# A two-layer transformer on one core: the softmax sums divided out per head group instead of per pair of groups, layer-norm copies kept in their stream, and seven planner constants changed

## The chip, the cores and the metric

The kernel runs on one core of a Trainium2 chip. The metric is the device time of one execution in microseconds (us); three executions of the kernel before took 896.95, 897.54 and 895.75 us, median 896.95. TensorE is called PE (its weight loads PEld), VectorE DVE, ScalarE ACT, GpSimd POOL, and the queue from which SyncE issues transfers SP.

## The reference

Two layers with shared weights; each layer is attention and then a feed-forward block, both with layer norm ahead of them and a residual around them. The sequence has 2048 rows of width 448; there are 16 heads of 28 columns; the hidden width is 1792.

```python
x = x + A(layernorm(x), A_wqkv, A_wo)
x = x + B(layernorm(x), B_w1, B_b1, B_w2, B_b2)
x = x + A(layernorm(x), A_wqkv, A_wo)
x = x + B(layernorm(x), B_w1, B_b1, B_w2, B_b2)

# A: q, k, v = split(x @ wqkv); p = softmax(q @ k.T * 28 ** -0.5); return (p @ v) @ wo
# B: h = relu(x @ w1 + b1); return (h * h) @ w2 + b2
```

## The kernel before, in words

**Order of the work.** The order of instructions on every engine is written by a planner (`Planner`, lines 124 to 214) that runs while the program is built. Each piece of work is an `Op` with an engine, an estimated duration, dependencies and buffers that it acquires (`acq`) and releases (`rel`). Ops stand in streams, and of one stream only the next Op can be chosen. The planner takes, again and again, the Op with the earliest possible start, and among equals that of the stream with the lowest number: 0 for scores, 1 for the exponentials on ACT, 2 for probabilities times values, 3 for normalization, 3.5 (`EV`) for copies out of PSUM, 4 and more for the chains described below. On the chip each engine then works through its queue in exactly this order.

**Attention.** The queries are cut into blocks of 256 rows (list `blocks`, line 242); the last 256 rows of layer 1 are two blocks of 128. A pass is one block of queries, one group of four heads, and a range of keys. Its score tiles of 128x512 are called units here; there are 2048 units over both layers, some 32 to a whole pass. `s_stream` (line 745) takes three units at a time into one PSUM tile of 1536 columns; `e_stream` (line 824) takes their exponential on ACT in one instruction (L833); `p_stream` (line 931) multiplies by the values (L981), whose fifth row block of ones gives the softmax sums as well, and evicts the result (L1004, L1006).

**Units on DVE.** Where `apart` (line 703) allows it, the third unit of a group goes to DVE, which computes the exponential with a polynomial: one instruction at L891, three at L908, one at L903 and the closing one at L914, which frees the scratch set. ACT then has a group of 1024 columns. `apart` refuses when fewer than `STOP` units are left, when no scratch set is free, or when DVE was busy over the last 12 planned us for more than a share `BUSY` = 0.95; the share is `LOW` = 0.6 when `behind` (line 688) says that the chains lag behind a line through the units given by `LINES` and `MARGIN`. The rest of a unit (`a_rest`) starts at a late priority and is raised to `V_LAST` = 1.8, ahead of `p_stream`, once `V_AGE` groups have gone by or once the scores have gone `V_PAST` units beyond the end of the unit's pass (line 897).

**Normalization.** When a pass ends its block and group, the result `oT_sb` holds 28 rows of values and a row of sums for each of four heads. Ahead of the last block of a layer, the sums go by DMA into a tile `dn` spread over 128 partitions (`spread`, L1079), are inverted on DVE (L1084), go to DRAM (`away`, L1090), come back broadcast to the rows of each head as `rec` (`back`, L1098), and DVE multiplies (L1103). `norm_pair` does this for two groups together, from one `oT_sb` tile with both; there are 30 such pairs. The last block of a layer goes through `norm_stream`: a matmul with `sel` copies the sums to all rows (L1046), then come a reciprocal (L1052) and a multiply (L1057).

**Chains.** When all four groups of a block are normalized, `chain` (line 1115) does its output projection, residual, layer norm, hidden layer (L1156 is the ReLU, L1160 the square) and second matrix; in layer 0 the next layer's Q, K and V follow. In `layernorm` the transposed rows are copied out of PSUM (L505); this copy is a stream of its own with number `EV` (line 508). PSUM gives `R_m`, two banks that accumulators, projections and transposes share.

**Buffers.** There are 11 tiles of exponentials (`NPT`), `NOS` tiles of `oT_sb`, and two of `rec`.

Of the kernel before, what the change touches and what calls it, by code (L numbers as in the profile page):

```python
# [11 lines left out]
DT = mybir.dt  # L12
AF = mybir.ActivationFunctionType
ALU = mybir.AluOpType
P = 128
# [20 lines left out]
DCLK = 0.2  # L36
OWN = 2
HALF = 320
LINES = ((280, 1312, 7.8), (1440, 2040, 7.0))
MARGIN = 2.0  # L40
LOW = 0.6
TURNS = 1
ENDU = 100
# [12 lines left out]
V_PRIO = 6.0  # L56
V_LATE = 3.6
V_LAST = 1.8
V_AGE = 6
V_PAST = 2  # L60
OWN3 = 0
FIRST = 90
V_FIRST = 9.2
# [7 lines left out]
BUSY = 0.95  # L71
SPAN = 12.0
NPT = 11
NOS = 3
AEND = 8
HOT = 0.9
MORE = 3
# [8 lines left out]
THIRD = 1  # L86
NL = 0
NLP = 3.8
STOP = 90
HSTOP = 0  # L90
CHUNK = 2
EV = 3.5
# [125 lines left out]
def kernel(  # L218
# [187 lines left out]
    def bank(o, name):  # L406

        if o.res in R_m:
            return ps_m[R_m.index(o.res)].tile([P, 512], DT.float32, name=name, tag="m")[:, :]
        return ps_sc.tile([P, 3 * 512], DT.float32, name="sc", tag="sc")[:, 0:512]  # L410


    def pools_now(early=False):
        return (*R_m, R_sc) if early or len(s_left) == 0 else R_m
# [39 lines left out]
    def layernorm(t0, nt, deps_of, early=False, mv=None, place=None):  # L454
# [26 lines left out]
        xnT = box["x"]  # L481
        ends = []
        todo = []

        def turn(p0, own, xs):
            box = {}

            def tr(e, xs=xs):
                tp = bank(t, "tp").bitcast(DT.bfloat16).rearrange("p (c q) -> p c q", c=NDC)
                box["t"] = tp  # L490
                for k, (xn, _) in enumerate(xs):
                    for dc in range(NDC):
                        nc.tensor.transpose(out=tp[:, dc, k * P:(k + 1) * P],
                                            in_=xn[:, dc * P:(dc + 1) * P], identity=ident[:, :])
            t = Op("PE", 0.07 * NDC * len(xs), tr, deps=[x[1] for x in xs],
                   acq=pools_now(early) if early else spare(1))
            yield t

            def ev(e, p0=p0, w=len(xs) * P):
                tp = box["t"]  # L500
                dst = xnT[:, :, p0 * P:p0 * P + w]
                if e == "ACT":
                    nc.scalar.copy(out=dst, in_=tp[:, :, 0:w])
                else:
                    nc.vector.tensor_copy(out=dst, in_=tp[:, :, 0:w])  # L505
            o = Op("DVE", 0.12 + 0.3 * len(xs), ev, deps=[t], rel=t, sets=[("xT", t0 + p0)] if early else ())
            ends.append(o)
            pl.spawn(EV, iter([o, Op("DVE", 0.0, None, deps=[t], rel=own)]))

        wide = 1 if single else 2  # L510
        for p0 in range(0, nt, wide):
# [18 lines left out]
            while todo:  # L530
                p0, own, xs = todo.pop(0)
                yield from turn(p0, own, xs)
        return xnT, own_xt, ends

    def mm_tile(subs, evac, ev_dur, deps, any_engine=False, sets=(), early=False, post=(), acq=None):
# [343 lines left out]
    def a_unit(gi, x, src, unit, l):  # L879
# [14 lines left out]
                apart_from(gi, t)  # L894
        c = Op("DVE", 0.69, take, deps=[("s", gi)], acq=sets_of(unit), rel=x)
        yield c
        pl.spawn(lambda now: V_LAST if e_now[1] - gi >= V_AGE or at[0] > ends_at[unit[0]] + V_PAST else V_LATE if now > c.end + V_WAIT else V_PRIO if gi > FIRST else V_FIRST, a_rest(gi, c, box, unit, (b0, b1, b2, b3)))

    def a_rest(gi, c, box, unit, bs):
        b0, b1, b2, b3 = bs  # L900
# [24 lines left out]
        yield o  # L925

    norm_done = {}
    pairs = {}
    oTn_of = {}

    def p_stream():


        for pi, (l, qb, g, kbs, first, last) in enumerate(passes):
# [58 lines left out]
                yield o  # L993
            res = {}
            def ev(e, box=box, first=first, last=last, g=g, res=res, n=n, l=l, qb=qb):
                pair = pairs.get((l, qb, g // 2))
                src = box["t"][:, 0:n]
                if last:
                    dst = res["t"] = pair["t"][:, g % 2, :]
                    dst = dst[:, 0:n]  # L1000
                else:
                    dst = part(l, qb, g)
                if first:
                    nc.vector.tensor_copy(out=dst, in_=src)  # L1004
                else:
                    nc.vector.tensor_tensor(out=dst, in0=src, in1=part(l, qb, g), op=ALU.add)  # L1006
            if last and (l, qb, g // 2) not in pairs:
                def both(e, l=l, qb=qb, g=g):
                    pairs[l, qb, g // 2]["t"] = osp.tile([P, 2, QR], DT.float32, name="oT_sb")
                pairs[l, qb, g // 2] = {"own": Op("DVE", 0.0, both, acq=R_os), "ev": [], "res": []}  # L1010
                yield pairs[l, qb, g // 2]["own"]
            pair = pairs[l, qb, g // 2] if last else None
            oe = Op("DVE", 0.15 + n / 930, ev, deps=[o], rel=box["o"])
            yield oe
            if last:
                pair["ev"].append(oe)
                pair["res"].append((g, res))
                if qb == len(blocks[l]) - 1:
                    pl.spawn(3, norm_stream(l, qb, g, res, oe, pair))
                elif len(pair["ev"]) == 2:  # L1020
                    pl.spawn(3, norm_pair(l, qb, g - g % 2, pair))

    def norm_start(l, qb):
        if (l, qb) not in oTn_of:
            def take(e):
                oTn_of[l, qb][0] = np_.tile([P, G, QR], DT.bfloat16, name="oTn")
            oTn_of[l, qb] = [None, Op("DVE", 0.0, take, acq=R_on)]
            yield oTn_of[l, qb][1]

    def norm_end(l, qb, m, gs):  # L1030

        norm_done.setdefault((l, qb), []).extend([m] * gs)
        if len(norm_done[l, qb]) == G:
            pl.spawn(LASTP if (l, qb) == (1, len(blocks[1]) - 1) else NLP + 0.1 * (qb - len(blocks[1])) if l == 1 and qb >= len(blocks[1]) - NL else 4 + 0.1 * qb, chain(l, qb))

    def norm_stream(l, qb, g, res, oe, pair):


        t0, nt = blocks[l][qb]
        n = nt * P  # L1040
        box = {}
        yield from norm_start(l, qb)

        def den(e):
            box["t"] = bank(d, "den")
            nc.tensor.matmul(box["t"][:, 0:n], lhsT=sel[:, :], rhs=res["t"][:, 0:n], start=True, stop=True)  # L1046
        d = Op("PE", 0.1 + n * 4 / 2400, den, deps=[oe], acq=pools_now())
        yield d

        def rcp(e):  # L1050
            box["r"] = rp.tile([P, 2, QR], DT.float32, name="rec")[:, 0, :]
            nc.vector.reciprocal(out=box["r"][:, 0:n], in_=box["t"][:, 0:n])  # L1052
        r = Op("DVE", n * 0.0066, rcp, deps=[d], rel=d, acq=R_rec)
        yield r

        def mul(e):
            nc.vector.tensor_tensor(out=oTn_of[l, qb][0][:, g, 0:n], in0=res["t"][:, 0:n],  # L1057
                                    in1=box["r"][:, 0:n], op=ALU.mult)
        m = Op("DVE", 0.13 + n / 930, mul, deps=[r, oTn_of[l, qb][1]])
        yield m  # L1060
        yield Op("DVE", 0.0, None, deps=[m], rel=r)
        pair.setdefault("mul", []).append(m)
        if len(pair["mul"]) == 2:
            yield Op("DVE", 0.0, None, deps=[m], rel=pair["own"])
        norm_end(l, qb, m, 1)

    def norm_pair(l, qb, g, pair):


        n = blocks[l][qb][1] * P  # L1070
        box = {}
        yield from norm_start(l, qb)
        w = n // DHP
        both = pair["t"][:, :, 0:n]

        def spread(e):
            box["d"] = sp.tile([P, 2, QR // DHP], DT.float32, name="dn")
            for i in range(2):
                nc.sync.dma_start(out=box["d"][:, i, 0:w], in_=both[DH::DHP, i, :])  # L1079
        d1 = Op("DMA", 0.9, spread, deps=pair["ev"], lat=1.0)  # L1080
        yield d1

        def rcp(e):
            nc.vector.reciprocal(out=box["d"][:, :, 0:w], in_=box["d"][:, :, 0:w])  # L1084
        r1 = Op("DVE", 0.33, rcp, deps=[d1])
        yield r1

        def away(e):
            box["s"] = dp.tile([P, 2 * w], DT.float32, name=f"scr{w}")[:, :].rearrange("p k -> (p k)")
            nc.sync.dma_start(out=box["s"].rearrange("(i p j) -> p i j", i=2, p=P), in_=box["d"][:, :, 0:w])  # L1090
        d2 = Op("DMA", 0.4, away, deps=[r1], lat=-0.5)
        yield d2

        def back(e):
            box["r"] = rp.tile([P, 2, QR], DT.float32, name="rec")
            for i in range(2):
                src = box["s"][i * P * w:(i + 1) * P * w].rearrange("(h k) -> h k", h=G)
                nc.sync.dma_start(out=box["r"][:, i, 0:n], in_=src.unsqueeze(1).to_broadcast([G, DHP, n]))  # L1098
        r = Op("DMA", 0.9, back, deps=[d2], acq=R_rec, lat=2.7)
        yield r  # L1100

        def mul(e):
            nc.vector.tensor_tensor(out=oTn_of[l, qb][0][:, g:g + 2, 0:n], in0=both,  # L1103
                                    in1=box["r"][:, :, 0:n], op=ALU.mult)
        m = Op("DVE", 0.13 + 2 * n / 930, mul, deps=[r, oTn_of[l, qb][1]], rel=pair["own"])
        yield m
        yield Op("DVE", 0.0, None, deps=[m], rel=r)
        norm_end(l, qb, m, 2)

    def add_to_x(tb, lo=0, hi=D):  # L1110
        def f(e, t):
# [149 lines left out]
```

## Time and profile before

| What | Value |
|---|---|
| median of three executions | 896.95 us |
| profiled execution, its own time | 896.95 us |
| its span, first to last instruction | 895.2 us |
| ACT busy | 876.9 us (98%) |
| DVE busy | 794.5 us (89%) |
| PE busy | 832.6 us (93%) |
| granted TensorE clock | 0.998 |
| exponentials on ACT with 1536 / 1024 columns | 555 / 128 |
| units computed on DVE | 127 |

Busy time is the union over an engine's instructions; consecutive ones overlap, so that the sum of single durations is larger than the busy time. Idle time of an engine that does not set the end costs nothing. Scores are repeated as filler on PE where the planner expects it to have room, so PE's busy time is not all needed work.

### The profile page before, as it was taken

The page shows a single profiled execution, that of the slowest core. Times are in us where ns is not written, and L with a number is a line of the kernel's source. Part 1 is how long each engine was busy: PE and PEld are TensorE (multiplying, and loading weights), DVE is VectorE, ACT ScalarE, POOL GpSimd, SP SyncE. Part 2 cuts the span into 40 slices and gives each one's busy share as a digit, 9 for nine tenths or more (in the row PEclk, how much of TensorE's full clock was granted, in tenths as well). Part 3 has the DMA queues.
Part 4 walks back from the last instruction along what each step waited for, and adds up shares of the span by engine and source line. Part 5 has one row for each costly group of instructions (what it writes and reads, how often), then busy time and mean ns, then how long its engine had stood idle before and what let it go on. Part 6 is the DMA issues. An engine that isn't in the chain of part 4 may idle for free.

```text
span 895.2 us, 29099 instructions
## 1 busy us (share of the span) xinstructions
PE 832.6 (93%) x12829; PEld 459.1 (51%) x12829; DVE 794.5 (89%) x1575; ACT 876.9 (98%) x704; POOL 39.0 (4%) x98
## 2 busy tenths in 40 slices
PE   8999999999999999999989998888999999999998
PEld 4555654554545545454454554444544544545566
DVE  7988999999889999999999999899898999989654
ACT  8999999999999999999999999999999999999994
POOL 3100000000000000100000000001000000000000
PEclk9999999999999999999999999999999999999999
DMA  9100100000000000000000000011000000000100
GB/s 259 41 3 3 27 17 12 14 14 15 14 2 15 15 14 14 12 10 9 2 1 3 2 2 2 3 39 39 14 13 19 20 25 24 15 10 17 32 19 13
DMA packets 33916, 18.43 MB, mean 21 GB/s; under 512 B 18875, under 2 KB 33340, under 8 KB 33789
## 3 DMA queue, kind: packets, MB, share of 16 engines
q1 hardware_dynamic: 33788, 16.58, 6.6%
q8 instruction: 100, 1.64, 0.8%
q14 instruction: 28, 0.22, 0.1%
HBM read 14.26 MB, written 2.07 MB: 18 GB/s over the span
## 4 chain that ended last, share of the span: by engine, by line
ACT 69%; issue 12%; PE 12%; DVE 5%; DMA 1%; SPq 1%; POOL 0%; DVEq 0%; ACTq 0%
ACT pt L833 69%; PE sc L809 4%; PE mt L553 4%; PE oT L981 3%; PE sc L553 1%; DMA rec<-scr 1%; DVE v_h L908 1%; DVE r L1156 1%; DVE st L448 1%; DVE K_sb L908 1%; DMA x_sb<-in_A_x_dram 0%; PE mt L1210 0%; SPq L303 0%; DVE oTn L1103 0%; DVE x_sb L1112 0%
## 5 line engine op out<-in xcount | busy, mean ns | idle before, releaser
L833 ACT ACTIVATE pt<-sc 128x1536 bf16<-128x1536 f32 (+1 forms) x683 | 863.9, 1565 | 2.9 <-PE sc L809 2.4
L809 PE MATMUL sc<-Q_sb,K_sb 32*128 32x256 bf16 (+1 forms) x5848 | 325.3, 265 | 53.5 <-ACT pt L833 47.3
L809 PEld LDWEIGHTS <-K_sb 32*128 32x128 bf16 x5848 | 157.5, 92 | 229.9 <-issue 200.9
L981 PE MATMUL oT<-pt,V_sb 128*32 128x256 bf16 (+1 forms) x4094 | 152.9, 269 | 0.6 <-DVE xnT L505 0.3
L553 PE MATMUL mt<-xnT,w 128*128 128x256 bf16 (+1 forms) x896 | 119.0, 271 | 1.9 <-DVE xnT L505 0.8
L981 PEld LDWEIGHTS <-V_sb 128*32 128x32 bf16 x4352 | 92.2, 96 | 46.7 <-issue 43.1
L908 DVE SCALAR_TENSOR_TENSOR K_sb<-K_sb 128x512 f32<-128x512 uint16 x165 | 112.9, 684 | 0.9 <-PE mt L553 0.2
L908 DVE SCALAR_TENSOR_TENSOR v_h<-v_h,v_i 128x512 f32<-128x512 f32 x144 | 98.2, 682 | 0.6
L553 PEld LDWEIGHTS <-w 128*128 128x128 bf16 x952 | 78.6, 98 | 36.5 <-issue 28.1
L1156 DVE TENSOR_SCALAR r<-mt 128x512 bf16<-128x512 f32 x106 | 72.2, 681 | 15.1 <-PE mt L553 14.8
L553 PE MATMUL mt<-w,V_sb 128*128 128x448 bf16 (+1 forms) x274 | 66.7, 352 | 0.0
L891 DVE TENSOR_SCALAR v_i<-sc 128x512 int32<-128x512 f32 x72 | 49.3, 685 | 9.7 <-PE sc L809 9.3
L1112 DVE TENSOR_TENSOR x_sb<-x_sb,mt 128x448 bf16<-128x448 bf16 (+1 forms) x63 | 38.2, 610 | 13.5 <-PE mt L553 13.5
L908 DVE SCALAR_TENSOR_TENSOR v_h<-v_i 128x512 f32<-128x512 uint16 x72 | 49.1, 682 | 0.5
L470 POOL TENSOR_TENSOR ve<-mv,eps_t 128x2 f32<-128x2 f32 (+1 forms) x34 | 8.8, 260 | 842.2 <-DVE mv L449 842.2
L1210 PE MATMUL mt<-xn,ident 128*128 128x448 bf16 x130 | 43.5, 357 | 0.5 <-DVE x_sb L1112 0.3
L891 DVE TENSOR_SCALAR K_sb<-sc 128x512 int32<-128x512 f32 x55 | 37.6, 684 | 5.5 <-PE sc L809 5.3
L448 DVE BATCH_NORM_STATS2 st<-x_sb 128x6 f32<-128x448 bf16 x64 | 39.4, 615 | 2.0 <-DMA x_sb<-in_A_x_dram 1.8
L553 PEld LDWEIGHTS <-V_sb 128*128 128x128 bf16 x302 | 24.8, 98 | 25.7 <-issue 11.2
L1160 DVE TENSOR_TENSOR V_sb<-r 128x512 bf16<-128x512 bf16 (+1 forms) x73 | 30.2, 414 | 2.8 <-ACT r L1154 2.2
L914 DVE SCALAR_TENSOR_TENSOR V_sb<-v_h,v_e 128x512 bf16<-128x512 f32 x46 | 31.3, 682 | 0.3
L553 PE MATMUL mt<-wo,oTn 128*128 128x448 bf16 x128 | 30.5, 355 | 0.1
(103 smaller groups left out, 734.8 us busy)
## 6 DMA issues: line engine op xcount, KB each, us to landing
rec<-scr SPq DMA_DIRECT2D x56, 128.0 KB
x_sb<-in_A_x_dram SPq DMA_DIRECT2D x8, 224.0 KB
out_dram<-x_sb SPq DMA_DIRECT2D x15, 112.0 KB
w<-in_B_w_dram SPq DMA_DIRECT2D x1, 1568.0 KB
w<-in_B_w_dram SPq DMA_DIRECT2D x1, 1344.0 KB
dn<-oT_sb SPq DMA_DIRECT2D x56, 4.0 KB
V_sb<-in_A_wqkv_dram SPq DMA_DIRECT2D x4, 168.0 KB
scr<-dn SPq DMA_DIRECT2D x28, 8.0 KB
```

The costliest lines, as they stand in the source:

```text
L448: nc.vector.bn_stats(out=st[:, :], in_=x_sb[:, t0 + j, :])
L553: nc.tensor.matmul(box["t"][:, c0:c0 + n], lhsT=lhsT() if callable(lhsT) else lhsT, rhs=rhs, start=a, stop=b)
L809: nc.tensor.matmul(dst[k][:, i * nt * P:(i + 1) * nt * P], lhsT=K_sb[l][rows, g, (kb + i) * P:(kb + i + 1) * P], rhs=Q_sb[rows, g, t0 * P: ...
L833: t = nc.scalar.activation(out=pt[:, 0:n], in_=gbuf[gi]["sc"][:, 0:n], func=AF.Exp, scale=float(np.log(2.0)) * 2.0 ** -FRAC)
L891: t = nc.vector.tensor_scalar(out=box["i"], in0=two(src), scalar1=EXP_BIAS, scalar2=EXP_LOW, op0=ALU.add, op1=ALU.max)
L908: nc.vector.scalar_tensor_tensor(out=box["h"], in0=box["f"] if begin else box["h"], scalar=b, in1=box["f"], op0=ALU.add, op1=ALU.mult)
L914: nc.vector.scalar_tensor_tensor(out=box["two"](pd), in0=box["h"], scalar=b0, in1=box["e"].bitcast(DT.bfloat16), op0=ALU.add, op1=ALU.mult)
L981: nc.tensor.matmul(box["t"][DHP * hh:DHP * hh + DHP, 0:n], lhsT=V_sb[l][:, kb + i, 4 * g + hh, :], rhs=p[:, c0:c0 + n], start=begin and kb ...
L1112: nc.vector.tensor_tensor(out=x_sb[:, tb, lo:hi], in0=x_sb[:, tb, lo:hi], in1=t[:, 0:hi - lo], op=ALU.add)
L1156: nc.vector.tensor_scalar(out=r[:, 0:w], in0=t[:, 0:w], scalar1=0.0, scalar2=None, op0=ALU.max)
L1160: nc.vector.tensor_tensor(out=h[:, 0:w // n, :], in0=r, in1=r, op=ALU.mult)
L1210: nc.tensor.matmul(t[:, 0:D], lhsT=ident[:, :], rhs=xns[0][:, 0:D], start=True, stop=True)
```

## The change

Three things change.

1. `norm_pair` goes; `norm_stream` serves all blocks. Ahead of the last block of a layer each group has its own spread, reciprocal, away, back and multiply, on tiles of half the size. `osp` has `NOS` = 4 tiles of one group in place of 3 tiles of two.
2. In `layernorm` the copies out of PSUM are yielded at the end of the layer norm's own stream, with that stream's number, and no longer spawned with number 3.5.
3. Constants: `LINES` for layer 0 from 7.8 to 8.0 blocks, `MARGIN` 2.0 to 4.0, `V_AGE` 6 to 5, `V_PAST` and its condition removed, `NOS` 3 to 4, `STOP` 90 to 80.

```diff
-LINES = ((280, 1312, 7.8), (1440, 2040, 7.0))
-MARGIN = 2.0
+LINES = ((280, 1312, 8.0), (1440, 2040, 7.0))
+MARGIN = 4.0
-V_AGE = 6
-V_PAST = 2
+V_AGE = 5
-NOS = 3
+NOS = 4
-STOP = 90
+STOP = 80
...
             ends.append(o)
-            pl.spawn(EV, iter([o, Op("DVE", 0.0, None, deps=[t], rel=own)]))
+            evs.extend([o, Op("DVE", 0.0, None, deps=[t], rel=own)])
...
+        yield from evs
         return xnT, own_xt, ends
...
-        pl.spawn(lambda now: V_LAST if e_now[1] - gi >= V_AGE or at[0] > ends_at[unit[0]] + V_PAST else V_LATE if now > c.end + V_WAIT else ...
+        pl.spawn(lambda now: V_LAST if e_now[1] - gi >= V_AGE else V_LATE if now > c.end + V_WAIT else ...
...
-            oe = Op("DVE", 0.15 + n / 930, ev, deps=[o], rel=box["o"])
+            oe = Op("DVE", 0.15 + n / 930, ev, deps=[o], rel=box["o"], acq=R_os if last else None)
             yield oe
             if last:
-                pair["ev"].append(oe)
-                pair["res"].append((g, res))
-                if qb == len(blocks[l]) - 1:
-                    pl.spawn(3, norm_stream(l, qb, g, res, oe, pair))
-                elif len(pair["ev"]) == 2:
-                    pl.spawn(3, norm_pair(l, qb, g - g % 2, pair))
+                pl.spawn(3, norm_stream(l, qb, g, res, oe))
...
+            def spread(e):
+                box["d"] = sp.tile([P, QR // DHP], DT.float32, name="dn")
+                nc.sync.dma_start(out=box["d"][:, 0:w],
+                                  in_=res["t"][DH::DHP, 0:n])
+            d1 = Op("DMA", 0.5, spread, deps=[oe], lat=1.0)
+            yield d1
+            def rcp(e):
+                nc.vector.reciprocal(out=box["d"][:, 0:w], in_=box["d"][:, 0:w])
+            r1 = Op("DVE", 0.25, rcp, deps=[d1])
+            yield r1
+            def away(e):
+                box["s"] = dp.tile([P, w], DT.float32, name=f"scr{w}")
+                nc.sync.dma_start(out=box["s"][:, :], in_=box["d"][:, 0:w])
+            d2 = Op("DMA", 0.4, away, deps=[r1], lat=-0.5)
+            yield d2
+            def back(e):
+                box["r"] = rp.tile([P, QR], DT.float32, name="rec")
+                src = box["s"][:, :].rearrange("(h a) j -> h (a j)", h=G)
+                nc.sync.dma_start(out=box["r"][:, 0:n], in_=src.unsqueeze(1).to_broadcast([G, DHP, n]))
+            r = own = Op("DMA", 0.5, back, deps=[d2], acq=R_rec, lat=2.7)
+            yield r
         def mul(e):
             nc.vector.tensor_tensor(out=oTn_of[l, qb][0][:, g, 0:n], in0=res["t"][:, 0:n],
                                     in1=box["r"][:, 0:n], op=ALU.mult)
-        m = Op("DVE", 0.13 + n / 930, mul, deps=[r, oTn_of[l, qb][1]])
+        m = Op("DVE", 0.13 + n / 930, mul, deps=[r, oTn_of[l, qb][1]], rel=oe)
```

More of the change, by code (lines that the diff above doesn't have):

```diff
@@ L483, in layernorm @@
         todo = []
+        evs = []
         def turn(p0, own, xs):
@@ L896, in a_unit @@
         yield c
-        pl.spawn(lambda now: V_LAST if e_now[1] - gi >= V_AGE or at[0] > ends_at[unit[0]] + V_PAST else V_LATE if now > c.end + V_WAIT else V_PRIO if gi > FIRST else V_FIRST, a_rest(gi, c, box, unit, (b0, b1, b2, b3)))
+        pl.spawn(lambda now: V_LAST if e_now[1] - gi >= V_AGE else V_LATE if now > c.end + V_WAIT else V_PRIO if gi > FIRST else V_FIRST, a_rest(gi, c, box, unit, (b0, b1, b2, b3)))
     def a_rest(gi, c, box, unit, bs):
@@ L927 @@
     norm_done = {}
-    pairs = {}
     oTn_of = {}
@@ L995, in ev @@
             def ev(e, box=box, first=first, last=last, g=g, res=res, n=n, l=l, qb=qb):
-                pair = pairs.get((l, qb, g // 2))
                 src = box["t"][:, 0:n]
                 if last:
-                    dst = res["t"] = pair["t"][:, g % 2, :]
+                    dst = res["t"] = osp.tile([P, QR], DT.float32, name="oT_sb")
                     dst = dst[:, 0:n]
@@ L1006, in ev, with norm_stream @@
                     nc.vector.tensor_tensor(out=dst, in0=src, in1=part(l, qb, g), op=ALU.add)
[L1007 to L1012, printed above, removed]
-            oe = Op("DVE", 0.15 + n / 930, ev, deps=[o], rel=box["o"])
+            oe = Op("DVE", 0.15 + n / 930, ev, deps=[o], rel=box["o"], acq=R_os if last else None)
             yield oe
             if last:
-                pair["ev"].append(oe)
-                pair["res"].append((g, res))
-                if qb == len(blocks[l]) - 1:
-                    pl.spawn(3, norm_stream(l, qb, g, res, oe, pair))
-                elif len(pair["ev"]) == 2:
-                    pl.spawn(3, norm_pair(l, qb, g - g % 2, pair))
-    def norm_start(l, qb):
+                pl.spawn(3, norm_stream(l, qb, g, res, oe))
+    def norm_stream(l, qb, g, res, oe):
+        t0, nt = blocks[l][qb]
+        n = nt * P
+        box = {}
+        tail = qb == len(blocks[l]) - 1
         if (l, qb) not in oTn_of:
@@ L1028, in norm_start, with den, rcp @@
             yield oTn_of[l, qb][1]
[L1030 to L1054, printed above, removed]
+        if tail:
+            def den(e):
+                box["t"] = bank(d, "den")
+                nc.tensor.matmul(box["t"][:, 0:n], lhsT=sel[:, :], rhs=res["t"][:, 0:n], start=True, stop=True)
+            d = Op("PE", 0.1 + n * 4 / 2400, den, deps=[oe], acq=pools_now())
+            yield d
+            def rcp(e):
+                box["r"] = rp.tile([P, QR], DT.float32, name="rec")
+                nc.vector.reciprocal(out=box["r"][:, 0:n], in_=box["t"][:, 0:n])
+            r = Op("DVE", n * 0.0066, rcp, deps=[d], rel=d, acq=R_rec)
+            own = r
+            yield r
+        else:
+            w = n // DHP
+            def spread(e):
[4 more added lines that the diff above has]
+            yield d1
+            def rcp(e):
+                nc.vector.reciprocal(out=box["d"][:, 0:w], in_=box["d"][:, 0:w])
[7 more added lines that the diff above has]
+            def back(e):
+                box["r"] = rp.tile([P, QR], DT.float32, name="rec")
+                src = box["s"][:, :].rearrange("(h a) j -> h (a j)", h=G)
+                nc.sync.dma_start(out=box["r"][:, 0:n], in_=src.unsqueeze(1).to_broadcast([G, DHP, n]))
+            r = own = Op("DMA", 0.5, back, deps=[d2], acq=R_rec, lat=2.7)
+            yield r
@@ L1058, in mul @@
                                     in1=box["r"][:, 0:n], op=ALU.mult)
-        m = Op("DVE", 0.13 + n / 930, mul, deps=[r, oTn_of[l, qb][1]])
+        m = Op("DVE", 0.13 + n / 930, mul, deps=[r, oTn_of[l, qb][1]], rel=oe)
         yield m
[L1061 to L1108, printed above, removed]
@@ L1110, in add_to_x @@
+        yield Op("DVE", 0.0, None, deps=[m], rel=own)
+        norm_done.setdefault((l, qb), []).append(m)
+        if len(norm_done[l, qb]) == G:
+            pl.spawn(LASTP if (l, qb) == (1, len(blocks[1]) - 1) else NLP + 0.1 * (qb - len(blocks[1])) if l == 1 and qb >= len(blocks[1]) - NL else 4 + 0.1 * qb, chain(l, qb))
     def add_to_x(tb, lo=0, hi=D):
```

## The prediction

> **What bounds the kernel now.** I read the page's engine totals and its chain of waits first, then the waits of ACT, then the groups with their shapes kept apart, then windows and stretches in order of time.
>
> ```profile
> PE 832.6 (93%) x12829; PEld 459.1 (51%) x12829; DVE 794.5 (89%) x1575; ACT 876.9 (98%) x704; POOL 39.0 (4%) x98
> ...
> ACT 69%; issue 12%; PE 12%; DVE 5%; DMA 1%; SPq 1%; POOL 0%; DVEq 0%; ACTq 0%
> ...
> L833 ACT ACTIVATE pt<-sc 128x1536 bf16<-128x1536 f32 (+1 forms) x683 | 863.9, 1565 | 2.9 <-PE sc L809 2.4
> ```
>
> The exponentials keep ACT busy for 863.9 us of 895.2, and ACT stood idle ahead of them for 2.9 us in all. So the time is three parts: an opening of some 20 us, a body in which ACT never waits, and an end after the last exponential. The body shortens only when units go to DVE.
>
> ```profile
> L833 ACT ACTIVATE pt<-sc 128x1536 bf16<-128x1536 f32 x555 | 775.8, 1644 | 2.8 <-PE sc L809 2.4 <-ACT pt L833 0.2
> L833 ACT ACTIVATE pt<-sc 128x1024 bf16<-128x1024 f32 x128 | 147.6, 1223 | 0.1
> L1103 DVE TENSOR_TENSOR oTn<-oT_sb,rec 128x512 bf16<-128x512 f32 x28 | 19.1, 684 | 1.6 <-DMA rec<-scr 1.6
> L1084 DVE RECIPROCAL dn<-dn 128x16 f32<-128x16 f32 x28 | 6.8, 244 | 0.9 <-DMA dn<-oT_sb 0.9
> L1057 DVE TENSOR_TENSOR oTn<-oT_sb,rec 128x256 bf16<-128x256 f32 x4 | 1.6, 410 | 0.0
> L1084 DVE RECIPROCAL dn<-dn 128x8 f32<-128x8 f32 x2 | 0.4, 188 | 0.0
> ```
>
> Neighbours overlap, so a price is the distance from one start to the next. In order of time, ACT near the end and DVE in the body:
>
> ```profile
> 834.13 44.27 ACT L833 ACTIVATE pt<-sc 128x1536 bf16<-128x1536 f32 x33
> ```
>
> ```profile
> 506.50 0.68 DVE L891 TENSOR_SCALAR K_sb<-sc 128x512 int32<-128x512 f32 x1
> 507.09 0.68 DVE L908 SCALAR_TENSOR_TENSOR v_h<-v_i 128x512 f32<-128x512 uint16 x1
> 507.69 0.42 DVE L903 TENSOR_SCALAR v_e<-v_i 128x512 int16<-128x512 int16 x1
> 508.03 0.68 DVE L571 TENSOR_SCALAR Q_sb<-mt 128x512 bf16<-128x512 f32 x1
> ```
>
> A wide exponential costs 44.27/33 = 1.34 us; the 128 narrow ones share 863.9 - 555 x 1.34 = 119 us, 0.93 each. One unit more on DVE makes one wide group narrow and saves 0.41 us. A unit costs DVE five instructions of 0.60 and one of 0.33: 3.3 us.
>
> The windows say how much DVE has left:
>
> ```profile
> 20.00:834.00 814.00, 761.07 (x11542) 412.89 (x11533) 746.83 (x1452) 812.48 (x646) 28.11 (x68) 1.00 0.06 15
> ...
> 800.00:840.00 40.00, 37.82 (x696) 21.63 (x694) 32.92 (x63) 40.00 (x33) 0.00 (x0) 1.00 0.09 25
> ```
>
> Columns are PE, PEld, DVE, ACT and POOL busy. DVE works 746.83 of 814 us (91.7%) in the body, near the planner's cap of 95%. DVE is therefore the second bound: each 3.3 us that the change takes from it costs ACT 0.41.
>
> **Part one: one group at a time.** Per pair, DVE now has a 512-wide multiply and a 16-wide reciprocal (0.60 + 0.16, start to start), afterwards two 256-wide multiplies and two 8-wide reciprocals (256-wide copies and multiplies start 0.33 apart, the 8-wide reciprocal of 856.94 us was followed after 0.12): 2 x 0.45 = 0.90, so 0.14 more. Thirty pairs: 4.2 us, 1.3 units, **+0.5 us**. Bounds: 0 if it falls into DVE's idle 67 us; by full durations (684 + 244 against 2 x 410 + 2 x 188, 0.27 each) 8 us, 2.4 units, +1.0.
>
> [...]
>
> On SP a pair issues two spreads, one away and two backs; afterwards it is two of each: 30 issues more, of 0.36 us (`scr` at 582.82), some 11 us over the run. No engine but DVE waits on these: 1.6 us for `rec`, 0.9 for `dn`. But SP issues in order, and an `away` that waits for a reciprocal holds back the spread of the next group. I take 0 and keep the bound in the third rival. NOS gives four groups in flight, where there were six.
>
> **Part two: the layer-norm copies, V_AGE and V_PAST.** The 34 copies at L505 (0.60 each) had number 3.5, ahead of late units (3.6) and chains; with 4 and up they stand behind both, and the transposed rows hold one of the two shared PSUM banks meanwhile. Behind each queue the hidden matmuls, then the ReLUs on DVE. In the opening they compete only with projections' evictions of 0.6 us and under; I take 0 there, bounds -0.3 and +0.6. A unit of a finished pass was raised when the scores were two units past its end; now only its age raises it, five groups, some 6.3 us. `p_stream` waits for it, behind that the accumulator's bank and its eviction on DVE. Against that, units that end no pass are raised one group (1.27 us) sooner and free their scratch set sooner. No row prices this. What it moves is the share of DVE in use: one percent of 814 us is 8.1 us, 2.4 units, 1.0 us. Bounds: up to the 95% cap, 3.3 percent, less the 4.2 us of part one, -2.7 us; two percent lost, +2.0. I take one percent lost, **+1.0**, since two of the three edits put waiting work later.
>
> **Part three: lines, margin, STOP.** Units pass at 2048/858 = 2.4 per us from 20 us on. By 480 us layer 0 has run some 50 ReLUs (7 a block), so between 6.4 and 7 blocks; its line stands at 6.1 before and after (7.8 x 0.793 - 2/20.2, 8 x 0.793 - 4/20.2): no effect, 0. In layer 1 at 800 us there are 35 ReLUs, 4.6 to 5 blocks, and the line falls from 4.78 to 4.64: here it bites. Chains may lag 2 counts more before DVE units are refused, and STOP lets units start 10 units (4 us) later. DVE in 800 to 840 us has 32.92 busy, 3.9 under the mean 36.9 of the windows from 40 to 800: 1.2 units, **-0.5** (bounds 0 and three units, -1.2).
>
> What the chains then owe is due at the end, where PE is full:
>
> ```profile
> 864.64 0.42 DVE L1103 TENSOR_TENSOR oTn<-oT_sb,rec 128x256 bf16<-128x256 f32 x1
> ```
>
> ```profile
> 871.15 0.93 PE L553 MATMUL mt<-wo,oTn 128*128 128x448 bf16 x4
> ...
> 882.47 2.81 PE L553 MATMUL sc<-w,V_sb 128*128 128x448 bf16 x14
> 885.15 0.40 PE L493 MATMUL tp<-ident,xn 128*128 128x128 bf16 x4
> 886.33 1.05 PE L553 MATMUL mt<-xnT,w 128*128 128x128 bf16 x16 [0.79 <-DVE xnT L505]
> ```
>
> Block 14's normalized rows are ready at 865.06, and their projection starts only at 871.15: PE was at the block before. Its second matrix, 2.8 counts, takes 2.81 us and ends just ahead of the last block's transposes. So a count is about 1 us of PE, 2 counts push up to 2 us into the end, and the idle 0.79 us at 886.33 takes some of it back: **+1.1** (bounds 0 and +2).
>
> **Sum:** 0.5 + 1.0 - 0.5 + 1.1 = +2.1. The profiled execution took 896.95 us, 1.75 over its span, and equals the median: 899.0 us.
>
> **Rivals.**
> *No change that can be told* (0.2%, 1.8 us, is about what a measurement of this kernel can tell). The chains do not use the margin, since their order is set by when passes end, and earlier raising by age pays for later raising at pass ends. Then part one and STOP are left: +0.5 - 0.2, 897.3. For it: ACT's body is untouched. Against: the backlog on PE before 871.15.
> *Faster.* Age 5 frees the scratch sets sooner, and DVE fills to its cap: -2.7, and -0.5 from STOP and margin, with no backlog at the end: 893.8 at full, 894.9 with two thirds. It decides if the body holds 131 units or more, 4 more than now. Against: part one takes DVE time, and the copies at 3.5 fed the chains.
> *Slower by stalls of ACT.* Where layer 1's passes end every 3.3 us (575 to 597 us: evictions at 575.01, 577.14, 578.49, 581.60, 584.83, 588.81), a pair took from 577.14 to the multiply at 590.36, 13 us. Four groups in flight cover 4 x 3.3 = 13 us, no more; six covered 20. If a single takes 16 us, as the next pair did (581.60 to 598.21), each round of four loses 3 us, and the twelve passes with three rounds 9; 11 tiles of exponentials cover some. ACT idle of 5 us: 902. It decides if a group holds its tile over 13 us. For it: SP's order. Against: ACT idles in 600 to 640 by 0.5 us only, and a single's own spreads and backs are half as many.
>
> **How the numbers follow.** My forecast 0.40, no change 0.36, stalls 0.12, faster 0.12. Slower therefore 0.52, same 0.36, faster 0.12. The forecast's own range is 898.75 to 901. The low end, 896.2, takes in no change and the mild half of faster; the high end, 902.0, all upper bounds of the body and the end (1.0 + 2.0 + 2.0 is +5.0), and half of the stalls.
>
> **What would show it.** Units at L891: 125 to 127 if parts one and two hold, with the body's DVE share 90 to 91% plus the added work; 131 or more speaks for the faster rival. L1103 goes, 60 multiplies and 60 small reciprocals come. After the last exponential now 16.8 us remain; 17.9 are expected, with block 14's second matrix ending after 885.3 less the shift of the body. Waits of ACT for scores beyond 3 us, or of DVE evictions around 575 to 600 us, speak for stalls. The prediction is wrong if the end is unchanged and DVE keeps its 127 units.

## The result and the profile after

The changed kernel takes 901.94 us (median of four, 901.12 to 902.50) beside 897.25 us for the kernel before (four runs, 895.75 to 899.36): 1.0050 times as long, 95% interval 1.0028 to 1.0072. The profiled execution took 901.12 us with a span of 899.3 us, 4.1 us over the span before.

The page of the changed kernel, engines, chain and exponentials:

```profile
PE 830.2 (92%) x12759; PEld 455.7 (51%) x12759; DVE 796.7 (89%) x1629; ACT 877.6 (98%) x704; POOL 39.4 (4%) x98
...
ACT 73%; issue 13%; PE 9%; DVE 4%; SPq 0%; DMA 0%; POOL 0%; ACTq 0%
...
L834 ACT ACTIVATE pt<-sc 128x1536 bf16<-128x1536 f32 (+1 forms) x683 | 864.5, 1579 | 3.2 <-PE sc L810 2.8
```

ACT is as full as it was: 864.5 us of exponentials against 863.9, with 3.2 us of waits against 2.9. The groups with their shapes kept apart show the normalization as the diff has it, and one unit fewer on DVE (126: 127 narrow groups, one of them the last group of the run):

```profile
L834 ACT ACTIVATE pt<-sc 128x1536 bf16<-128x1536 f32 x556 | 776.5, 1656 | 3.2 <-PE sc L810 2.8
L834 ACT ACTIVATE pt<-sc 128x1024 bf16<-128x1024 f32 x127 | 146.3, 1240 | 0.0
L1064 DVE TENSOR_TENSOR oTn<-oT_sb,rec 128x256 bf16<-128x256 f32 x60 | 24.8, 415 | 0.4 <-DMA rec<-scr 0.4
L1047 DVE RECIPROCAL dn<-dn 128x8 f32<-128x8 f32 x56 | 10.6, 192 | 0.0
```

The body's window (columns PE, PEld, DVE, ACT, POOL) has DVE at 744.77 us of 814, where it was 746.83:

```profile
20.00:834.00 814.00, 755.63 (x11430) 407.99 (x11429) 744.77 (x1495) 812.10 (x644) 28.43 (x68) 1.00 0.05 15
```

So the body hardly moved. The end did. ACT in order of time, first before, then after; the second line of each is block 7's first ReLU on ACT:

```profile
836.91 41.49 ACT L833 ACTIVATE pt<-sc 128x1536 bf16<-128x1536 f32 x31
879.22 0.60 ACT L1154 ACTIVATE r<-mt 128x512 bf16<-128x512 f32 x1 [0.82 <-PE mt L553]
```

```profile
834.02 45.20 ACT L834 ACTIVATE pt<-sc 128x1536 bf16<-128x1536 f32 x34
884.41 0.60 ACT L1117 ACTIVATE r<-sc 128x512 bf16<-128x512 f32 x1 [5.18 <-PE sc L554]
```

The last exponential ends at 878.40 before and 879.22 after, 0.8 us later. From there to the end of the span it is 16.8 us before and 20.1 after: 3.3 of the 4.1 us. Block 7 (rows 1792 to 1919 of layer 1; block 8 is the last) begins its hidden layer 0.82 us after the last exponential before, and 5.18 us after it now. PE in order of time says what stood ahead of it. Before:

```profile
871.15 0.93 PE L553 MATMUL mt<-wo,oTn 128*128 128x448 bf16 x4
...
875.93 0.40 PE L493 MATMUL tp<-ident,xn 128*128 128x128 bf16 x4 [0.34 <-DVE xn L520]
...
876.84 0.49 PE L553 MATMUL mt<-xnT,w 128*128 128x128 bf16 x6
```

After:

```profile
869.29 0.93 PE L554 MATMUL mt<-wo,oTn 128*128 128x448 bf16 x4
...
870.83 1.11 PE L554 MATMUL mt<-w,V_sb 128*128 128x448 bf16 x5
872.21 0.93 PE L554 MATMUL mt<-w,V_sb 128*128 128x448 bf16 x4
...
877.02 0.40 PE L810 MATMUL sc<-Q_sb,K_sb 32*128 32x128 bf16 x8 [0.27 <-ACT pt L834]
...
877.91 0.36 PE L554 MATMUL mt<-b2w,one 128*128 128x448 bf16 x1
...
880.92 1.11 PE L554 MATMUL mt<-w,V_sb 128*128 128x448 bf16 x5
881.86 0.39 PE L493 MATMUL sc<-ident,xn 128*128 128x128 bf16 x4
...
883.32 1.05 PE L554 MATMUL sc<-xnT,w 128*128 128x128 bf16 x16 [0.32 <-DVE xnT L505]
```

Block 7's projection (`wo,oTn`) even comes earlier (869.29 for 871.15), but its transposes (L493) come at 881.86, six us later than before: between the two lies the whole second matrix of block 6 (`w,V_sb`). Its first half stands between scores that come at ACT's pace (868.96 to 877.02 us in six steps, 1.34 us each). Its second half begins at 877.91, behind the last scores of the run (877.02), and from there to the transposes PE's rows follow each other without a wait. Block 6 is late: its last ReLU on DVE starts at 869.20, where it was 857.64.

```profile
857.64 0.69 DVE L1156 TENSOR_SCALAR r<-mt 128x512 bf16<-128x512 f32 x1 [0.16 <-PE mt L553]
```

```profile
869.20 0.68 DVE L1119 TENSOR_SCALAR r<-mt 128x512 bf16<-128x512 f32 x1
```

The lag grows on the way: block 5's last residual is at 843.71 where it was 838.96 (4.8 us), block 6's first ReLU at 855.66 where it was 848.06 (7.6 us), its last 11.6 us later.

### The profile page after: what moved, and what is told of

The parts are those of the page before. It is cut to its first block, busy times and chain, and to the rows that moved or that the text cites. A ratio compares the mean times of both kernels' runs of the same rounds, so it can differ in the third digit from the quotient of the medians.

```text
span 899.3 us, 29011 instructions
## 1 busy us (share of the span) xinstructions
PE 830.2 (92%) x12759; PEld 455.7 (51%) x12759; DVE 796.7 (89%) x1629; ACT 877.6 (98%) x704; POOL 39.4 (4%) x98
## 4 chain that ended last, share of the span: by engine, by line
ACT 73%; issue 13%; PE 9%; DVE 4%; SPq 0%; DMA 0%; POOL 0%; ACTq 0%
ACT pt L834 73%; PE mt L554 4%; PE sc L810 3%; PE oT L981 1%; DVE st L447 1%; DVE K_sb L909 1%; PE sc L554 1%; DVE v_h L909 0%; SPq L302 0%; DMA x_sb<-in_A_x_dram 0%; DVE x_sb L1075 0%; DVE v_i L892 0%; DVE K_sb L892 0%; PE tp L493 0%; PE mt L1173 0%
## 5 line engine op out<-in xcount | busy, mean ns | idle before, releaser
L834 ACT ACTIVATE pt<-sc 128x1536 bf16<-128x1536 f32 (+1 forms) x683 | 864.5, 1579 | 3.2 <-PE sc L810 2.8
L810 PE MATMUL sc<-Q_sb,K_sb 32*128 32x256 bf16 (+1 forms) x5768 | 320.6, 265 | 58.3 <-ACT pt L834 50.8
L810 PEld LDWEIGHTS <-K_sb 32*128 32x128 bf16 x5768 | 153.7, 92 | 236.6 <-issue 205.9
L554 PE MATMUL mt<-w,V_sb 128*128 128x448 bf16 (+1 forms) x288 | 69.8, 352 | 0.0
L1173 PE MATMUL mt<-xn,ident 128*128 128x448 bf16 x140 | 47.5, 359 | 0.6
L554 PEld LDWEIGHTS <-V_sb 128*128 128x128 bf16 x302 | 24.9, 98 | 24.6 <-issue 10.6
L1003 DVE COPY oT_sb<-oT 128x256 f32<-128x256 f32 (+1 forms) x48 | 19.0, 396 | 16.3 <-PE oT L981 16.2
```

The costliest lines, as they stand in the source:

```text
L554: nc.tensor.matmul(box["t"][:, c0:c0 + n], lhsT=lhsT() if callable(lhsT) else lhsT, rhs=rhs, start=a, stop=b)
L810: nc.tensor.matmul(dst[k][:, i * nt * P:(i + 1) * nt * P], lhsT=K_sb[l][rows, g, (kb + i) * P:(kb + i + 1) * P], rhs=Q_sb[rows, g, t0 * P: ...
L834: t = nc.scalar.activation(out=pt[:, 0:n], in_=gbuf[gi]["sc"][:, 0:n], func=AF.Exp, scale=float(np.log(2.0)) * 2.0 ** -FRAC)
L1173: nc.tensor.matmul(t[:, 0:D], lhsT=ident[:, :], rhs=xns[0][:, 0:D], start=True, stop=True)
```

## The experiments

Two theories were set against each other. A: the parts cost what their own work costs, and MARGIN and STOP let the chains owe more at the end. B: any edit makes the planner write another order, the order before is a favourable one, and what counts is how that order falls out at a few places. One table for all runs. The ratio is to the kernel before as timed beside that run; the other columns are from the profiled execution. "Units" are units on DVE; "end" is the time from the last exponential to the end of the span; "block 7" is the delay of its first ReLU on ACT behind the last exponential; "waits" are the waits of the exponentials from 22 us on.

| Kernel | time, ratio to before (95%) | units | last exponential | end | block 7 | waits |
|---|---|---|---|---|---|---|
| before | 1 | 127 | 878.4 | 16.8 | 0.8 | 1.0 |
| after | 1.0050 (1.0028 to 1.0072) | 126 | 879.2 | 20.1 | 5.2 | 1.6 |
| b_split | 0.9992 (0.9983 to 1.0001) | 127 | 877.1 | 16.8 | 0.8 | 0.2 |
| b_stop80 | 1.0021 (1.0013 to 1.0030) | 129 | 877.3 | 19.8 | 4.7 | 1.1 |
| b_lines | 1.0057 (1.0045 to 1.0069) | 129 | 876.7 | 21.7 | 7.2 | 0.4 |
| b_age | 1.0109 (1.0096 to 1.0122) | 125 | 880.4 | 24.6 | 8.4 | 2.0 |
| b_evac | 1.0076 (1.0061 to 1.0090) | 128 | 880.2 | 22.0 | 7.7 | 3.3 |
| b_singles | 1.0138 (1.0125 to 1.0151) | 124 | 884.9 | 21.1 | 5.4 | 7.1 |
| b_over081 | 1.0183 (1.0161 to 1.0206) | 128 | 888.1 | 23.6 | 7.7 | 11.8 |
| a_over081 | 1.0078 (1.0064 to 1.0092) | 128 | 877.0 | 25.0 | 8.6 | 0.9 |
| a_reorder | 1.0032 (1.0020 to 1.0044) | 131 | 880.5 | 16.9 | 0.8 | 4.6 |
| b_reorder | 0.9987 (0.9978 to 0.9995) | 131 | 876.5 | 16.8 | 0.8 | 1.6 |
| a_half6 | 1.0038 (1.0025 to 1.0051) | 126 | 878.8 | 19.5 | 4.7 | 1.3 |
| b_half6 | 1.0006 (0.9995 to 1.0016) | 127 | 876.6 | 16.8 | 0.8 | 0.2 |

The last exponential of kernels with the same order and units scatters by over 1 us between profiled executions (before, b_split and b_half6: 878.4, 877.1, 876.6); the end does not (16.8 in all three).

Much of this scatter goes with the clock that PE was granted. Beside the experiments the kernel before was timed 57 times: 33 executions with a mean granted clock of 1.000 took 895.6 us on average, 23 with 0.998 took 896.7, and the one with 0.994 took 899.7. In the profiled execution of before the clock is 0.81 in 212 to 216 us and 0.76 in 216 to 220, and ACT waits 0.8 us for scores at 217.42; b_split, in the same order, has 1.00 there and no wait. The changed kernel has such a stretch at 396 to 404 us (0.76 and 0.81) with a wait of 0.9 us, so that it and before stay comparable. Other rows of the table hold more of it. All 3.3 us of b_evac's waits lie in two such stretches, near 144 and 252 us. In the end the clock falls too, over four us to 0.50 in b_age and a_over081, to 0.58 in b_singles and to 0.66 in b_over081, where the other kernels keep 1.00 while PE works (in tenths, the page's last fortieth of the span stands at 8 in b_age and a_over081 and at 9 in all others): b_evac and b_over081 both begin block 7 7.7 us late, and their ends are 22.0 and 23.6. So the largest costs and ends here are not the order's waits alone. How much of them is the clock's, and what makes it fall, was not tested.

**Part one's own work, in the order of before (b_split).**

```diff
-            nc.vector.reciprocal(out=box["d"][:, :, 0:w], in_=box["d"][:, :, 0:w])
+            for i in range(2):
+                nc.vector.reciprocal(out=box["d"][:, i, 0:w], in_=box["d"][:, i, 0:w])
...
-            nc.vector.tensor_tensor(out=oTn_of[l, qb][0][:, g:g + 2, 0:n], in0=both, in1=box["r"][:, :, 0:n], op=ALU.mult)
+            for i in range(2):
+                nc.vector.tensor_tensor(out=oTn_of[l, qb][0][:, g + i, 0:n], in0=both[:, i, :], in1=box["r"][:, i, 0:n], op=ALU.mult)
```

The `away` transfer is split in the same way.

> The kernel before with its order of work kept: norm_pair stays, the planner is told the same durations, but each reciprocal of 16 columns is issued as two of 8, each away transfer as two, and each 512-wide multiply as two of 256. This is part one's own work without any reshuffling. Theory A (the parts' own work and what the chains owe at the end set the time): DVE gets 0.14 us more per pair, 4.2 us in all, the units stay 127, so ACT's body stays and the time moves by 0 to +0.5 us. Theory B (what counts is that any edit gives the planner another order): order kept, so 0 within 0.5 us. Only a rise of 1 us or more would say that the split itself costs what the forecast put at +0.5 to +1.0.

Measured: 895.49 beside 896.11 us, ratio 0.9992. Thirty multiplies, thirty reciprocals and thirty transfers more cost nothing that can be told, as long as the order stays: DVE busy rose from 794.5 to 796.7 us, and its idle time took that.

**STOP alone (b_stop80).**

```diff
-STOP = 90
+STOP = 80
```

> The kernel before with STOP 90 changed to 80 alone. Up to unit 1958, some 838 us, the order is that of before; after it up to two units more go to DVE. Theory A: the units save 0.41 us each on ACT (last exponential 0.4 to 0.8 us earlier), but take 3.3 us of DVE each while block 6 begins its hidden layer, so the stretch after the last exponential grows from 16.8 to 18 us or more: 0.5 to 2 us slower in all. Rival: DVE has 15 us idle between 838 and 878, the units fit there, the end stays at 16.8 us, and the time falls by 0.4 to 0.8 us.

Measured: 898.06 beside 896.11 us, 2.0 us slower, and the end is 19.8 us. This is the cleanest pair, since the order is the same up to some 838 us. DVE of this kernel in order of time:

```profile
838.98 0.68 DVE L891 TENSOR_SCALAR v_i<-sc 128x512 int32<-128x512 f32 x1
839.84 0.69 DVE L891 TENSOR_SCALAR K_sb<-sc 128x512 int32<-128x512 f32 x1 [0.18 <-PE sc L809]
...
850.47 0.68 DVE L505 COPY xnT<-tp 128x1024 bf16<-128x1024 bf16 x1
...
863.10 0.69 DVE L1156 TENSOR_SCALAR r<-mt 128x512 bf16<-128x512 f32 x1 [0.19 <-PE mt L553]
```

Two units more start at 838.98 and 839.84, block 6's transposed rows are copied at 850.47 instead of 845.47, its last ReLU comes at 863.10 instead of 857.64, and block 7 begins 4.7 us after the last exponential. What 5.5 us of delay to block 6 costs is 3.0 us at the end, for at most 0.8 us saved on ACT (two units of 0.41). The rival, that the units fit into idle time, is refuted.

**The other parts, each alone on the kernel before.**

```diff
-LINES = ((280, 1312, 7.8), (1440, 2040, 7.0))
-MARGIN = 2.0
+LINES = ((280, 1312, 8.0), (1440, 2040, 7.0))
+MARGIN = 4.0
```

> The kernel before with LINES 8.0 and MARGIN 4.0 alone (STOP stays 90). Theory A: no effect in layer 0; in layer 1 chains may lag two counts more, so one or two units more on DVE (0.4 to 0.8 us off the last exponential) and a stretch after it that is 1 to 3 us longer than 16.8: together 0.5 to 2.5 us slower, and block 6's last ReLU later than before's 857.6. Theory B: likewise slower, but not through the line alone: the order changes from the first place where a choice tips.

For b_age the diff's lines on V_AGE and V_PAST, for b_evac its lines on `evs`, for b_singles its normalization and NOS = 4, each without the rest.

> The kernel before with V_AGE 5 and without V_PAST alone. The forecast gave this, with the layer-norm copies, one percent of DVE's body: 2.4 units fewer, +1.0 us, the end as before at 16.8. Theory A: units 124 to 126, 0.4 to 1.3 us slower, the end unchanged. Theory B: the end too falls out anew, 18 to 24 us, so 2 to 8 us slower.

> The kernel before with the layer-norm copies kept in their stream alone. Theory A: within 1 us of before, end unchanged (34 copies, each at most some tenths of a us later). Theory B: 2 to 7 us slower, with a longer end.

> The kernel before with one head group normalized at a time and NOS 4 alone; layer-norm copies, V_AGE, V_PAST, lines, margin and STOP as before. The same DVE and SP work with before's order kept moved the time by -0.6 us, inside its interval. Theory A: so this costs at most 1 us, in up to two units. Theory B: 3 us or more slower, by a longer end or, by the forecast's rival, by waits of ACT of several us where layer 1's passes end every 3.3 us (575 to 640 us).

Measured: +0.57%, +1.09%, +0.76% and +1.38%. With STOP's +0.21% the five sum to 4.0%, and all together make 0.50%: the parts don't add, and none of their single costs is its share of the change. Theory A holds for b_lines in kind (two units more, a longer end, block 6's last ReLU at 867.42), but not in size: the end is 4.9 us longer where it said 1 to 3, and the time 5.0 where it said 0.5 to 2.5. For the other three it fails: it said an unchanged end for b_age and b_evac and at most 1 us for b_singles, and the ends are 21.1 to 24.6 us. b_singles is the plainest: its own work is free in b_split, and as a change of the order it costs 1.4%. It has 3 units fewer, a longer end, and one long wait of ACT, seen in its order of time on ACT and on PE:

```profile
574.47 5.97 ACT L833 ACTIVATE pt<-sc 128x1536 bf16<-128x1536 f32 x5 [7.14 <-PE sc L809]
```

```profile
570.80 1.52 PE L553 MATMUL mt<-xnT,wk 128*128 128x256 bf16 x8 [1.40 <-DVE xnT L505]
```

At this place layer 1's scores need the keys of layer 0's last block. They are projected at 570.80 here and evicted from 572.36 on; before they were evicted from 561.52, in the changed kernel from 555.88. So the wait is not the forecast's third rival (tiles of `oT_sb` where passes end), but a second deadline for a chain.

**An edit that means nothing, on both kernels.**

```diff
-OVER = 0.08
+OVER = 0.081
```

> The kernel before with the planner's estimate of how far neighbours on DVE overlap changed from 0.08 to 0.081 us. This means nothing for the work; it only tips close choices of the planner, and so gives another order. Theory A (own work and owed chains): within 1 us of before, units 126 to 128, since nothing in the work or in the line of the chains changed. Theory B (order before is a favourable one, and most orders are slower): 2 to 8 us slower, with the loss in the stretch after the last exponential (over 18 us against 16.8), in fewer units, or in waits of ACT.

> The changed kernel with the same meaningless edit (0.08 to 0.081). Theory A: within 1 us of the changed kernel, 901 to 903 us, stretch after the last exponential about 20 us. Theory B: anywhere from 897 to 906, as the end falls out.

Measured: 912.59 beside 896.11 us, and 903.33. One nanosecond in an estimate moved the kernel before by 1.8%, more than three times the change under study. It has one unit more than before and lost at both deadlines, with the granted clock at 0.993 to 0.996 in all five executions; its waits of ACT:

```profile
ACT pt L833 <- PE sc L809: 13.0, 8, 7.2
ACT r L1154 <- PE sc L553: 10.6, 4, 7.7
```

7.2 us fall where layer 1 starts (keys evicted from 571.73 on), and the end is 23.6 us. Theory A's "within 1 us" is refuted for before. For the changed kernel the same edit gives two units more, an earlier last exponential and an end 5 us longer, where theory A said about 20 us; the time is 1.4 us above that of the changed kernel.

**Other orders, chosen for where block 7 begins.** a_reorder is the whole change with OVER = 0.088 and SPAN = 13.0; b_reorder is the kernel before with OVER = 0.0912, SPAN = 13.0, MARGIN = 1.5, STOP = 95 and V_AGE = 7.

> The changed kernel with all three of its changes in place, and two settings of the planner's own estimates moved: the overlap of neighbours on DVE from 0.08 to 0.088 us, and the stretch over which DVE's load is averaged from 12 to 13 us. In this order 131 units go to DVE. Theory A (the changed parts cost what they cost): still 2 us or more slower than before, since singles, late copies, MARGIN 4 and STOP 80 are all there; the end stays near 20 us, and 4 units more take at most 1.6 us off. Theory B (the order decides): if block 7's ReLUs begin by 1 us after the last exponential, as in before, the end is 17 us again, and with 131 units the time falls to 895 to 897.5: no slower than before.

> The kernel before with the overlap at 0.0912 us, the averaged stretch at 13 us, MARGIN 1.5, STOP 95 and V_AGE 7: an order with 131 units on DVE. Theory B: with an end of 17 us and 4 units more than before, 894 to 895.5, up to 0.2% faster than before. Theory A says the same of the units, but nothing of why the end should stay.

a_reorder took 899.26 beside 895.99 us. Theory B is right on the end: with singles, late copies, MARGIN 4 and STOP 80 all in place, block 7 begins 0.82 us after the last exponential and the end is 16.9 us.

```profile
819.01 61.44 ACT L834 ACTIVATE pt<-sc 128x1536 bf16<-128x1536 f32 x47
881.27 0.60 ACT L1117 ACTIVATE r<-mt 128x512 bf16<-128x512 f32 x1 [0.82 <-PE mt L554]
```

It is wrong on the time, 895 to 897.5; there theory A's "2 us or more slower" came true, though not by the end that it gave as the reason. This order has 4.6 us of waits in the body (the longest 2.2 us, at 395 us, at a granted clock of 1.00), which cost more than four units more (1.6 us) bring. Whether the changed parts have a share in these waits stays open. So it is not shown that the changed kernel can be as fast as before, only that its longer end belongs to its order: with all its parts in place another order does not have it. b_reorder took 895.01 beside 895.99 us, 0.13% faster (interval 0.05 to 0.22%), and is the fastest kernel measured here: an end of 16.8 us, 131 units, the last exponential at 876.5.

**Is it the amount of PE's work that block 7 waits for (a_half6, b_half6)?** Both leave out the odd terms 1 to 11 of block 6's second matrix, on PE only:

```diff
                 for c0, n, lhsT, rhs, a, b, _ in part:
+                    if getattr(lhsT, "skip", False):
+                        continue
                     nc.tensor.matmul(box["t"][:, c0:c0 + n], lhsT=lhsT() if callable(lhsT) else lhsT, rhs=rhs,
                                      start=a, stop=b)
```

> The changed kernel with its order kept, but 12 of the 28 matmuls of block 6's second matrix (layer 1) left out; its rows 1536 to 1791 are therefore not the reference's. They lie between 870 and 882 us, some 0.2 us of PE each, 2.4 us together. If PE's owed work is what stands between the last exponential and block 7's hidden layer, its ReLUs on ACT (now 5.2 us after the last exponential) start 1.5 to 2.4 us earlier and the time falls by as much. If block 7 waits for something else (its own normalization, a bank, its layer norm), the time falls by less than 0.7 us.

> The kernel before with the same 12 matmuls of block 6's second matrix left out, order kept; rows 1536 to 1791 are not the reference's. In before these matmuls lie between 858 and 871 us, and block 7's projection follows at 871.15, six us after its normalized rows. The last block's chain cannot begin before the last exponential, so the end stays between 16 and 16.8 us and the time falls by 0.8 us at most, where the changed kernel gains 1.5 to 2.4.

a_half6 took 900.11 us (ratio 1.0038; the intervals of it and of the changed kernel overlap), with a span 1.0 us under the changed kernel's, 0.5 of it in the end. Block 7 begins 4.7 us after the last exponential instead of 5.2. Of the 2.4 us left out the span shows 1.0, which lies between the two cases. PE in order of time shows where the rest went:

```profile
875.54 0.55 PE L556 MATMUL mt<-w,V_sb 128*128 128x448 bf16 x2
876.55 0.40 PE L812 MATMUL sc<-Q_sb,K_sb 32*128 32x128 bf16 x8 [0.46 <-ACT pt L836]
...
877.45 0.36 PE L556 MATMUL mt<-b2w,one 128*128 128x448 bf16 x1
...
880.49 0.39 PE L493 MATMUL sc<-ident,xn 128*128 128x128 bf16 x4
```

Half of what was left out lies in the first half of the matrix, between scores that come at ACT's pace. There it leaves gaps: PE stands 0.46 us ahead of the scores until ACT frees their buffer. The other half, 1.2 us, lies behind the last scores, where PE works without a wait. There it counts: block 7's transposes come 1.73 us after the last exponential (880.49) instead of 2.64 (881.86), 0.9 us sooner. Some 0.4 us of that is lost again on DVE, whose queue has the last block's multiply and a residual ahead of the copy of these transposes, so that the copy starts at 881.86 instead of 882.85. So PE's owed work is a part of what block 7 waits for, but only the part behind the last scores. In before, leaving out the same work changed nothing (1.0006), as expected.

## Why the prediction was right, and where it was not

The forecast was 899.0 us, +2.1, slower at 0.52, with a range to 902.0; measured were 901.94 and +4.7. Direction and range held; the size was under half. That the range held is luck: 901.94 lies 0.06 us inside it and beyond the 898.75 to 901 of the forecast's own sum. The end went beyond its own bound of 2, and the body, with +0.8, stayed far below its bounds of 1.0 and 2.0.

**What bounds the kernel** held: ACT, then DVE, then the stretch behind the last exponential. To about 1 us, all kernels in the table differ only in units, waits of ACT and the end.

**Part one, +0.5:** too much. In before's order it is -0.6 us with an interval that includes 0 (b_split). In single durations the small instructions are dearer: of the 60 multiplies of 415 ns, 56 stand for 28 of 684, 23.2 us for 19.2. b_split shows that this does not reach the time here: its small instructions add 2.2 us to DVE's busy time (794.5 to 796.7), and DVE's idle time takes them. The third rival did not come true either: the changed kernel shows no wait of ACT between 560 and 640 us.

**Part two, +1.0 through DVE's share:** the body as a whole, parts one and two and the units of part three, was forecast at 0.5 + 1.0 - 0.5 = +1.0; the last exponential moved by +0.8 (126 units, DVE at 91.5%). The sum fits, within the scatter of 1 us; the reasons do not, so this is luck too. DVE's share went from 91.7 to 91.5%, not down by one percent, and the same edits alone (b_age, b_evac) cost 1.1 and 0.8%, mostly at the end, which the forecast had left out for this part.

**Part three, -0.5 of units:** not taken up; there are 126, though MARGIN or STOP alone brings two more (b_lines, b_stop80: 129).

**The end, +1.1 with bounds 0 and 2:** the term that was mis-sized; it measured +3.3. The step that failed is "a count is about 1 us of PE, 2 counts push up to 2 us into the end". (A count is the planner's measure of a chain's progress: a block of 256 rows in layer 1 has 14.2, of which 7 are its ReLUs and 5.6 its second matrix. The prediction's block 14, counted in rows of 128, is block 7 here.) Two counts are 2 us of PE, but at the pace of the chains in the body (7 ReLUs, 14.2 counts, in 40 us) they are 5.6 us of time. Block 5 was indeed 4.8 us late, which fits, though it is not shown that MARGIN made it so; block 6 then lost more, 11.6 us at its last ReLU. And block 7 waits not for two counts but for a place in PE's queue behind the whole second matrix of block 6. That is 2 x 2.8 us of PE, which takes the 11 us from 870.6 to 881.9: up to 877 because scores at ACT's pace stand between its matmuls, and from there, with other work, at PE's own pace (a_half6). b_stop80 has the same step at work in isolation: 5.5 us of delay to block 6, +3.0 us of end. Why the transposes were not put ahead of the second matrix is argued only: the chain of block 6 has the lower number, and one of the two shared banks is with its accumulator, the other with the pass; the transposes go to a score buffer (`sc`) once the scores are over. It wasn't tried.

**What the forecast had no case for** is that an edit's cost here can be mostly that of the other order which it sets off. This is shown for part one (its own work is free in b_split; b_singles, which has NOS = 4 as well, costs 1.4%) and for an edit that means nothing. Of the other parts only STOP was measured with the order kept, up to 838 us. Which part makes block 6 late in the changed kernel stays open: alone, each of the five edits lengthens the end, as the meaningless one does, and with other estimates all of them together do not (a_reorder). What is shown is the deadline: in all kernels whose block 7 begins by 0.8 us after the last exponential the end is 16.8 to 16.9 us, and in all where it begins 4.7 us or more after it, 19.5 to 25.0.

## What to carry to other kernels

Where a program writes the order, measure a meaningless edit first: here one nanosecond in an estimate was worth 1.8%, so the cost of an edit can be read only with the order kept (as in b_split), or over several orders. Look for the chains that have a deadline, here layer 0's last keys and block 6 ahead of the last exponential: work that slips cost nothing as long as block 7 could still begin 0.8 us after the last exponential, and some 3 to 8 us at the end where it could not. Compare the granted clock of the executions before a microsecond is put down to an edit. Price owed work by the pace at which the chain runs in that stretch, not by the busy time of its matmuls alone.

## What the runs showed of the hardware that was not expected

Thirty more instructions of each kind on DVE (256-wide multiplies of 0.42 us, 8-wide reciprocals of 0.17) and thirty more transfers raised DVE's busy time by 2.2 us only (794.5 to 796.7), against 4.2 worked out from starts and 8 from durations: short neighbours overlap more than the durations say, and the reciprocals more than the forecast's starts had it. In b_split the two reciprocals of a pair are followed 0.18 us after the first one's start (at 800.47 and 826.57 us), for the forecast's 0.24; the two multiplies after 0.67 to 0.68 (at 781.99, 808.54 and 834.49 us), for its 0.66. By these starts thirty pairs would add an estimated 2.9 us (0.18 + 0.675 against 0.16 + 0.60 before).

A short fall of PE's granted clock showed as a wait on ACT. In before the clock is 0.62 and 0.52 in the two windows from 214 to 218 us, after waits of PE of 0.73 and twice 0.23 us from 211.4 us on, and ACT loses 0.8 us at 217; the same order in b_split has a mean clock of 1.000 over its profiled execution and no wait of ACT for scores from 22 us on. So a fall can come in one execution and not in another, and what it costs here is about the 1 us between the executions at 0.998 and at 1.000.
